# Attention softmax: when the row sums are inverted, and on which engine

## The chip, the cores and the metric

One core of a Trainium2 chip. The metric is the device time of one execution in microseconds (us), the median of three. PE is the matrix engine, with PEld its weight loads; DVE, ACT and POOL are the vector, scalar and GpSimd engines; SP issues most of the DMAs. Each engine works through its own queue in the order in which it was written and waits where an operand isn't ready, so what stands behind a waiting instruction waits too.

## The reference

Causal attention with a decay bias over 4 batches of 8 heads, 576 rows of 64, followed by a gated MLP and a routed mixture of experts. The part at hand:

```python
scores = np.where(causal, -1000000000.0, scores + np.minimum(bias, 0.0))
scores = scores - np.max(scores, axis=-1, keepdims=True)
attn = np.exp(scores)
attn = attn / (np.sum(attn, axis=-1, keepdims=True) + 1e-09)
return np.matmul(attn, v).astype(np.float32)
```

## The kernel before

Attention runs over 32 heads g and, in each, over 5 query tiles i (128 rows each, the last one 64), so 160 tiles (g, i). Tile i has 128(i+1) columns of keys, the last one 576. For one tile:

- S: PE multiplies query and key rows into PSUM (`emit_S`, line 726).
- minimum: DVE copies the negated scores to the tile E, adds the mask and keeps the row minimum (line 424; for i = 4 in two halves, a and b).
- exponent: ACT takes the exponent in place and leaves the row sums in column i of `lsum` (line 432).
- add, reciprocal, scale: POOL adds 1e-9 to the sums (line 436), DVE inverts them (line 437), POOL multiplies E by them (line 440).
- T: PE transposes E (`emit_T`, line 458), ACT or DVE copies the result out of PSUM (lines 463 to 468).
- PV: PE multiplies by the values (`emit_PV`, line 490): the first two tiles of a head together, then the other three.

`A_steps(4)` holds a tile back for four tiles: T of tile (g, i) is written behind S of the fourth tile after it. E has one buffer for each i (two for i = 0). On top of that the early heads share the engines with other work: `split_f64` takes apart the first MLP weights (DMA, then lines 608 and 614 on ACT, 609, 612 and 615 on DVE, 613 on POOL), `emit_cum` makes the bias rows in head 4 (lines 230 to 239, on DVE and ACT), `emit_X` splits a pair of finished heads on POOL (lines 513 and 514), and from about 105 us on the MLP of a finished batch runs between the heads.

The order on each queue isn't the order of the program text: a scheduler sets it, by its own estimate of when each instruction is ready and by the place in the text. An instruction that is given as being behind another one (`behind`) stays behind it, and that alone makes it wait for nothing.

Of the kernel before, what the change touches and what calls it, by code (L numbers as in the profile page):

```python
# [13 lines left out]
ALU = mybir.AluOpType  # L14
# [19 lines left out]
def kernel(  # L34
# [19 lines left out]
    PE, ACT, DVE, POOL, SP = nc.tensor, nc.scalar, nc.vector, nc.gpsimd, nc.sync  # L54
# [7 lines left out]
    NQ = (S + 127) // 128  # L62
    QM = [min(128, S - 128 * i) for i in range(NQ)]
# [6 lines left out]
    NH = B * H  # L70
# [11 lines left out]
    def behind(x, name):  # L82

        tc.add_manual_dep(
            x.ins, name, mybir.DependencyInfo(mybir.DependencyClass.NoSync, mybir.DependencyReason.DATA), reason="after"
        )
# [8 lines left out]
    def ps(tag="ps", bufs=7):  # L95
        t = psum.tile([128, 512], F32, tag=tag, name=tag, bufs=bufs)
        return t
# [18 lines left out]
    def T(pool, shape, dt, tag, bufs=1):  # L116
        _n[0] += 1
        return pool.tile(shape, dt, tag=tag, name=f"{tag}_{_n[0]}", bufs=bufs)
# [42 lines left out]
    def warm_up(n):  # L161

        w = keep_warm[0]
        pw = rs()
        for _ in range(n):
            PE.matmul(pw[0:32].rearrange("p (a c) -> p a c", c=32), lhsT=w, rhs=w.unsqueeze(1).to_broadcast([128, 16, 32]), start=True, stop=True)
# [20 lines left out]
    def slot(z, dt=F32R):  # L187
        x = wsg[:, z, :]
        return x if dt == F32R else x.bitcast(dt)
# [36 lines left out]
    def emit_cum():  # L226
        R = 128 // NH
        s_sb = T(mp, [128, S], F32, "u2", bufs=5)[0:NH]
        dma(s_sb, s.rearrange("b h s -> (b h) s"))
        behind(DVE.tensor_scalar_max(out=s_sb, in0=s_sb, scalar1=0.0), hred[max(hred)].ins.name)  # L230
        cum = s_sb
        DVE.tensor_tensor_scan(out=cum, data0=one[0:NH], data1=s_sb, initial=0.0, op0=ALU.mult, op1=ALU.add)
        for P, i0, z0 in ((128, 0, 6), (NH, R, 8)):
            tmp = T(mp, [128, S], F32, "u2", bufs=5)
            ch = wsg[0:P, z0:z0 + 2, :]
            for a in range(P // NH):
                DVE.tensor_scalar(out=tmp[NH * a:NH * a + NH], in0=cum, scalar1=cum[:, 128 * (i0 + a):128 * (i0 + a) + 1], scalar2=None, op0=ALU.subtract)
            ACT.copy(out=ch[:, 0, :], in_=tmp[0:P])
            DVE.tensor_tensor(out=ch[:, 1, :], in0=tmp[0:P], in1=f32v(ch[:, 0, :]), op=ALU.subtract)
            dma(cum_d[:, NH * i0:NH * i0 + P, :].rearrange("z p s -> p z s"), ch)  # L240
# [22 lines left out]
    def prep_load(p):  # L263
        b, h0 = divmod(2 * p, H)
        for src, nm in ((q, "nq"), (k, "nk")):
            t = T(ap_, [96, 6, 2, D], F32, nm)
            for h in range(2):
                dma(t[:, :, h, :], src[b, h0 + h].rearrange("(r p) d -> p r d", p=96))
            nat[p, nm] = t
# [94 lines left out]
    def prep_asm(g):  # L364
        p, r = divmod(g, 2)
        dst = QK[buf[g]]
        t = Tst[p]
        rs = slice(64 * r, 64 * r + 64)
        dma(dst[64:KX, 3, :], cum_rows[g] if g >= GD else cumr[cblk(g):cblk(g) + 2 * NQ])
        if buf[g] not in selected:  # L370
            selected.add(buf[g])
            dma(dst[64:KX, 2, :], sel[64:KX])
        dma(dst[0:64, 0:3, :], t[rs, 0:3, :])
        dma(dst[0:64, 3, :], t[rs, 1, :])
        dma(dst[64:128, 0:2, :], t[rs, 0:4:3, :])
        if r == 1:
            Tst.pop(p)
# [24 lines left out]
    Et, lsum, hred = {}, {}, {}  # L402

    def emit_S(g, i):
        qk = QK[buf[g]] if g >= ND else None
        M = QM[i]
        N = 128 * i + M
        e = T(ap_, [128, 128 * (i + 1)], F32, f"E{i}", bufs=2 if i==0 else 1) if i < NQ - 1 else E4
        Et[g, i] = e
        nm = T(ap_, [128, 2], F32, "negm", bufs=6)  # L410
        halves = [(0, N)] if N <= 512 else [(0, HS), (HS, N)]
        for hi, (a, z) in enumerate(halves):
            pt = ps()
            n = z - a
            qs = slice(128 * i, 128 * i + M)
            if g < ND:
                t = Tst[g // 2]
                qh, ql = QZ[g]
                pairs = [(qh[:, qs], t[:, 1, a:z]), (qh[:, qs], t[:, 3, a:z]), (ql[:, qs], t[:, 1, a:z]), (slot(6 + g)[:, qs], cumr[:, a:z])]
            else:  # L420
                pairs = [(qk[:, 0, qs], qk[:, 1, a:z]), (qk[0:KX, 2, qs], qk[0:KX, 3, a:z])]
            mm3(pt[0:M, 0:n], pairs, True, True)
            m0 = 512 - 128 * i + a if z == N else 0
            hred[g] = DVE.tensor_tensor_reduce(  # L424
                out=e[0:M, a:z], in0=pt[0:M, 0:n], in1=zmask[0:M, m0:m0 + n], scale=-1.0,
                scalar=BIG if hi == 0 else nm[0:M, 0:1], op0=ALU.add, op1=ALU.min, accum_out=nm[0:M, hi:hi + 1],
            )
        last = len(halves) - 1
        if i == 0:
            lsum[g] = T(ap_, [128, 8], F32, "lsum", bufs=3)  # L430
        l = lsum[g]
        ACT.activation(out=e[0:M, 0:N], in_=e[0:M, 0:N], func=ACTF.Exp, scale=-1.0, bias=nm[0:M, last:last + 1], accum_out=l[0:M, i:i + 1])  # L432
        if i in LG:
            i0 = LG[i]
            c = slice(i0, i + 1)
            POOL.tensor_scalar(out=l[0:M, c], in0=l[0:M, c], scalar1=1e-9, scalar2=0.0, op0=ALU.add, op1=ALU.add)  # L436
            DVE.reciprocal(out=l[0:M, c], in_=l[0:M, c])  # L437
            for x in range(i0, i + 1):
                n = 128 * x + M
                POOL.tensor_scalar(out=Et[g, x][0:M, 0:n], in0=Et[g, x][0:M, 0:n], scalar1=l[0:M, x:x + 1], scalar2=1.0, op0=ALU.mult, op1=ALU.mult)  # L440

    ET = {}
    LG = {z: z for z in range(NQ)}

    def emit_T(g, i):
        e = Et.pop((g, i))
# [88 lines left out]
    def A_steps(LAG):  # L535
        fifo = []
        for n in range(NH * NQ):
            g, i = n // NQ, n % NQ
            p = g // 2
            if i == 0:  # L540
                for x in when:
                    if when[x] == g and g:
                        prep_asm(x)
            if g < len(WU) and WU[g]:
                warm_up(WU[g])
            emit_S(g, i)
            if (g, i) == EC0:
                emit_cum()
            yield 2 * max(107, (128 * i + QM[i]) * 0.42)
            fifo.append((g, i))  # L550
            if (g, i) == RS:
                prep_T(1, 0)
                prep_T(1, 1)
                prep_load(2)
                for x in when:
                    if when[x] == 0:
                        prep_asm(x)
            for p in range(1, NH // 2):
                if (when.get(2 * p) or g) - 1 == g and i in (3, 4):
                    prep_T(p, i - 3)  # L560
                    if i == 4 and p + 1 < NH // 2:
                        prep_load(p + 1)
                    yield 600
            if len(fifo) > LAG:
                yield from after(*fifo.pop(0))
        for x in fifo:
            yield from after(*x)
        emit_PV(NH - 1, 1)
        yield 1230
        emit_X(NH // 2 - 1)  # L570
        done_x[0] += 1
        yield 600
# [4 lines left out]
    def after(g, i):  # L577
        emit_T(g, i)
        yield 110 * (i + 1)
        if i == 2:  # L580
            emit_PV(g, 0)
            yield 860
        if i == 1 and g > 0:
            emit_PV(g - 1, 1)
            yield 1230
        if i == XI and g > 0 and g % 2 == 0:
            emit_X((g - 1) // 2)
            done_x[0] += 1
            yield 600
        if i == 1 and g + 2 < NH:  # L590
            prep_V(g + 2)
# [132 lines left out]
    def mm3(pt, pairs, first_, last_):  # L724
        n = len(pairs)
        ms = [PE.matmul(pt, lhsT=l, rhs=r, start=(first_ and x == 0), stop=(last_ and x == n - 1)) for x, (l, r) in enumerate(pairs)]  # L726
        return ms
# [415 lines left out]
    def fetch(dst, idx, n=NT):  # L1143
        return POOL.indirect_dma_start(
            out=dst, out_offset=None, in_=x2_d[0:n, :], in_offset=bass.IndirectOffsetOnAxis(ap=idx, axis=0),
            bounds_check=n - 1, oob_is_err=False,
        )
# [247 lines left out]
    A_COST, M_COST, O_COST = 45.0, 44.0, 13.0  # L1395
    A_pro()
    A = A_steps(4)
    w = W_steps()
    wg = list(WG)
# [45 lines left out]
    x = fetch(early["xg2"], ids[:, CAP - 1:CAP])  # L1445
# [36 lines left out]
```

## Time and profile before

| what | value |
|---|---|
| median of 3 runs | 802.25 us (800.07 to 802.88) |
| the profiled execution | 803.59 us, its span 801.8 us |
| PE busy | 763.7 us, 95% of the span |
| DVE busy | 532.6 us, 66% |
| ACT busy | 447.0 us, 56% |
| POOL busy | 347.4 us, 43% |

The profiled execution is 1.34 us above the median, and 1.8 us of it lie outside the span. PE is busy nearly all the time; the time that it isn't lies mostly in the first 150 us. A row of the timeline gives start, duration, engine, line, operation, tiles and shape; what stands in brackets is the idle time of that engine just before, and what ended it. A row with x2 is two instructions in a row, merged. The clock that was granted to PE is 1.00 at 2.4 GHz and 0.50 at 1.2 GHz.

### The profile page before, as it was taken

The page shows a single profiled execution, that of the slowest core. Times are in us where ns is not written, and L with a number is a line of the kernel's source. Part 1 is how long each engine was busy: PE and PEld are TensorE (multiplying, and loading weights), DVE is VectorE, ACT ScalarE, POOL GpSimd, SP SyncE. Part 2 cuts the span into 40 slices and gives each one's busy share as a digit, 9 for nine tenths or more (in the row PEclk, how much of TensorE's full clock was granted, in tenths as well). Part 3 has the DMA queues.
Part 4 walks back from the last instruction along what each step waited for, and adds up shares of the span by engine and source line. Part 5 has one row for each costly group of instructions (what it writes and reads, how often), then busy time and mean ns, then how long its engine had stood idle before and what let it go on. Part 6 is the DMA issues. An engine that isn't in the chain of part 4 may idle for free. (4 is left out here: it accounts for less than half of the span.)

```text
span 801.8 us, 14966 instructions
## 1 busy us (share of the span) xinstructions
PE 763.7 (95%) x4744; PEld 643.8 (80%) x4744; DVE 532.6 (66%) x1624; ACT 447.0 (56%) x1077; POOL 347.4 (43%) x629
## 2 busy tenths in 40 slices
PE   9887998999999999999999999998999999999994
PEld 4554687879988888988888877977898988988983
DVE  6668667678698788968788467767454534545530
ACT  5656668687574778745787325413545434545530
POOL 4678663677572568752487401004302121231110
PEclk9988999899999999999999999998999999999998
DMA  6999699974687949578763374312656464665520
GB/s 140 225 229 255 154 243 294 261 201 128 150 170 237 224 106 259 113 161 253 179 140 114 109 250 160 112 61 71 226 179 204 139 209 132 187 192 165 180 81 26
DMA packets 119604, 138.69 MB, mean 173 GB/s; under 512 B 69494, under 2 KB 82934, under 8 KB 119524
## 3 DMA queue, kind: packets, MB, share of 16 engines
q1 hardware_dynamic: 116196, 128.23, 60.2%
q0 software_dynamic: 3328, 9.48, 3.1%
q8 instruction: 39, 0.64, 0.3%
q14 instruction: 41, 0.34, 0.2%
HBM read 89.97 MB, written 22.15 MB: 140 GB/s over the span
## 5 line engine op out<-in xcount | busy, mean ns | idle before, releaser
L1131 DVE TENSOR_TENSOR wp<-wraw,wp 128x1024 fp32r<-128x1024 f32 x63 | 76.6, 1225 | 92.3 <-ACT wp L1130 92.2
L440 POOL TENSOR_SCALAR E<-E,lsum 128x128 f32<-128x128 f32 (+4 forms) x160 | 98.7, 619 | 37.2 <-DVE lsum L437 24.3
L432 ACT ACTIVATE E<-E,negm 128x128 f32<-128x128 f32 (+4 forms) x160 | 97.0, 607 | 23.7 <-DVE negm L424 20.3
L1130 ACT CAST wp<-wraw 128x1024 fp32r<-128x1024 f32 x64 | 66.5, 1048 | 63.4 <-DMA wraw<-in_moe_w_dram 58.7
L726 PE MATMUL ps<-xT,wp 128*128 128x288 f32 (+4 forms) x672 | 99.3, 308 | 0.0
L726 PEld LDWEIGHTS ps<-xT,wp 128*128 128x128 f32 x672 | 98.2, 189 | 0.8
L726 PE MATMUL ps<-wp,hT 128*128 128x512 f32 (+1 forms) x408 | 96.4, 395 | 0.0
L424 DVE CUSTOM_DVE_ANT_0 E<-ps,zmask 128x128 f32<-128x128 f32 (+4 forms) x160 | 75.2, 473 | 21.4 <-PE ps L726 20.6
L726 PEld LDWEIGHTS ps<-wp,hT 128*128 128x128 f32 (+1 forms) x408 | 75.4, 187 | 17.2
L726 PE MATMUL ps<-qk 128*128 128x128 f32 (+3 forms) x354 | 85.6, 337 | 3.5 <-DVE tst L356 1.7
L458 PE MATMUL ps<-ident,E 128*128 128x128 f32 (+1 forms) x480 | 75.2, 264 | 12.4 <-POOL E L440 6.3
L1205 POOL DMA_INDIRECT out_dram<-y,idsr x16 | 20.0, 1250 | 149.0 <-ACT y L1204 117.0
L436 POOL TENSOR_SCALAR lsum<-lsum 128x1 f32<-128x1 f32 (+1 forms) x160 | 38.4, 240 | 102.8 <-ACT E L432 94.1
L458 PEld LDWEIGHTS ps<-ident,E 128*128 128x128 f32 (+1 forms) x480 | 51.2, 140 | 24.5 <-POOL E L440 11.6
L726 PE MATMUL ps<-wsg,vg 128*128 128x288 f32 x448 | 67.7, 301 | 1.6 <-DVE etb L468 1.0
L490 PE MATMUL ps<-etb,vv 128*128 128x320 f32 (+5 forms) x340 | 63.0, 337 | 1.0 <-DVE negm L424 0.8
L726 PEld LDWEIGHTS ps<-wsg,vg 128*128 128x128 f32 x448 | 61.1, 189 | 3.2 <-DVE etb L468 1.3
L726 PEld LDWEIGHTS ps<-qk 128*128 128x128 f32 (+1 forms) x354 | 51.5, 173 | 13.5 <-issue 2.2
L490 PEld LDWEIGHTS ps<-etb,vv 128*128 128x128 f32 (+1 forms) x340 | 49.4, 178 | 14.1 <-issue 5.6
L726 PE MATMUL ps<-xh,w 128*128 128x288 f32 x256 | 57.3, 304 | 0.0
L726 PE MATMUL ps<-w,vg 128*128 128x512 f32 (+1 forms) x216 | 55.1, 399 | 0.0
L726 PE MATMUL ps<-w,xh 128*128 128x512 f32 (+1 forms) x160 | 52.4, 405 | 0.0
(327 smaller groups left out, 1585.4 us busy)
## 6 DMA issues: line engine op xcount, KB each, us to landing
wraw<-in_moe_w_dram SPq DMA_DIRECT2D x64, 512.0 KB
qk<-tst SPq DMA_DIRECT2D x28, 432.0 KB
w<-wv_d SPq DMA_DIRECT2D x16, 512.0 KB
w<-wo_d SPq DMA_DIRECT2D x16, 512.0 KB
qk<-tst SPq DMA_DIRECT2D x28, 288.0 KB
w<-wu_d SPq DMA_DIRECT2D x12, 512.0 KB
nq<-in_q_dram SPq DMA_DIRECT2D x32, 144.0 KB
nk<-in_k_dram SPq DMA_DIRECT2D x32, 144.0 KB
```

Source lines behind the costliest of these rows:

```text
L424: hred[g] = DVE.tensor_tensor_reduce(out=e[0:M, a:z], in0=pt[0:M, 0:n], in1=zmask[0:M, m0:m0 + n], scale=-1.0, scalar=BIG if hi == 0 else ...
L432: ACT.activation(out=e[0:M, 0:N], in_=e[0:M, 0:N], func=ACTF.Exp, scale=-1.0, bias=nm[0:M, last:last + 1], accum_out=l[0:M, i:i + 1])
L436: POOL.tensor_scalar(out=l[0:M, c], in0=l[0:M, c], scalar1=1e-9, scalar2=0.0, op0=ALU.add, op1=ALU.add)
L440: POOL.tensor_scalar(out=Et[g, x][0:M, 0:n], in0=Et[g, x][0:M, 0:n], scalar1=l[0:M, x:x + 1], scalar2=1.0, op0=ALU.mult, op1=ALU.mult)
L458: PE.transpose(pt[:, j * M:(j + 1) * M], e[0:M, 128 * j:128 * (j + 1)], ident[0:M, 0:M])
L490: PE.matmul(pt[0:128 if wide else 64, a:n], lhsT=l, rhs=et[0:kk, z, j, a:n] if g >= F4 else f32v(et[0:kk, 0, j, a:n]), start=(j == 0 and n ...
L726: ms = [PE.matmul(pt, lhsT=l, rhs=r, start=(first_ and x == 0), stop=(last_ and x == n - 1)) for x, (l, r) in enumerate(pairs)]
L1130: c = ACT.copy(out=w[:, 0, :], in_=r)
L1131: a = (POOL if (e, j) == (0, KD) else DVE).tensor_tensor(out=w[:, 1, :], in0=r, in1=f32v(w[:, 0, :]), op=ALU.subtract)
L1205: POOL.indirect_dma_start(out=of[:, :], out_offset=bass.IndirectOffsetOnAxis(ap=idx[0:n], axis=0), in_=y[0:n], in_offset=None, bounds_chec ...
```

## The change

The add goes from POOL to DVE, and add, reciprocal and scale are written one tile later: for tile (g, i) they are issued in the step of the next tile, and the add is put behind the next tile's minimum on DVE. Behind the last tile of the last head one call flushes what is left.

```diff
-        if i in LG:
-            i0 = LG[i]
-            c = slice(i0, i + 1)
-            POOL.tensor_scalar(out=l[0:M, c], in0=l[0:M, c], scalar1=1e-9, scalar2=0.0, op0=ALU.add, op1=ALU.add)
-            DVE.reciprocal(out=l[0:M, c], in_=l[0:M, c])
-            for x in range(i0, i + 1):
-                n = 128 * x + M
-                POOL.tensor_scalar(out=Et[g, x][0:M, 0:n], in0=Et[g, x][0:M, 0:n], scalar1=l[0:M, x:x + 1], scalar2=1.0, op0=ALU.mult, op1=ALU.mult)
+        unscaled.append((g, i))
+        scale_rows(LS, hred[g])
+
+    unscaled = []
+
+    def scale_rows(n, red):
+
+        while len(unscaled) > n:
+            g, i = unscaled.pop(0)
+            M = QM[i]
+            N = 128 * i + M
+            e = Et[g, i][0:M, 0:N]
+            l = lsum[g][0:M, i:i + 1]
+            x = DVE.tensor_scalar(out=l, in0=l, scalar1=1e-9, scalar2=0.0, op0=ALU.add, op1=ALU.add)
+            behind(x, red.ins.name)
+            DVE.reciprocal(out=l, in_=l)
+            POOL.tensor_scalar(out=e, in0=e, scalar1=l, scalar2=1.0, op0=ALU.mult, op1=ALU.mult)
 
     ET = {}
-    LG = {z: z for z in range(NQ)}
+    LS = 1
...
+        scale_rows(0, hred[NH - 1])
         for x in fifo:
             yield from after(*x)
```

The work of PE, ACT and SP stays the same; POOL has 160 instructions less and DVE 160 more. The scheduler also gives many of the others a new place. Three places of this follow. Line numbers of the changed kernel are up to 10 higher: 446, 448 and 449 are its add, reciprocal and scale, and 474, 618, 619, 622, 623 and 625 are 465, 608, 609, 612, 613 and 615 of before.

Place A, DVE in head 1, from the minimum of tile (1, 3) (128x512) on. Tile `vg` holds weights that a DMA brings. Before:

```order
L424 ISA E_89_496,negm_497<-ps,zmask_73 128x512
L424 ISA negm_497 128x1
L437 RECIPROCAL lsum_414<-lsum_414 128x1
L356 SCALAR_TENSOR_TENSOR tst_508<-ps,tst_508 128x288
L465 COPY etb_461<-ps 128x5x64
L359 TENSOR_TENSOR tst_508<-ps,tst_508 128x288
L609 TENSOR_SCALAR vg_420<-vg_420 128x512
L424 ISA E_32_104,negm_531<-ps,zmask_73 64x288
L424 ISA negm_531 64x1
L437 RECIPROCAL lsum_414<-lsum_414 128x1
```

Now:

```order
L424 ISA E_89_493,negm_494<-ps,zmask_73 128x512
L424 ISA negm_494 128x1
L446 TENSOR_SCALAR lsum_411<-lsum_411 128x1
L619 TENSOR_SCALAR vg_417<-vg_417 128x512
L356 SCALAR_TENSOR_TENSOR tst_505<-ps,tst_505 128x288
L474 COPY etb_458<-ps 128x5x64
L448 RECIPROCAL lsum_411<-lsum_411 128x1
L622 SCALAR_TENSOR_TENSOR vg_417<-vg_417 128x512
L424 ISA E_32_104,negm_528<-ps,zmask_73 64x288
```

The weight step (609, now 619) moved ahead of 356, of the copy of `etb` and of the reciprocal of tile (1, 2); 359 moved behind the minimum (1, 4a). The reciprocal of tile (1, 3), the last row of before, now comes 15 rows after the rows shown, behind the second half of the tile and the next two weight steps (619).

Place C, POOL in head 3, from the split of a weight (613, now 623) to the scale of tile (3, 4) (64x576). Before:

```order
L613 TENSOR_TENSOR vg_600<-vg_600,g_104_602 128x512
L440 TENSOR_SCALAR E_123_758<-E_123_758,lsum_715 128x256
L436 TENSOR_SCALAR lsum_715<-lsum_715 128x1 x2
L440 TENSOR_SCALAR E_127_779<-E_127_779,lsum_715 128x384
L440 TENSOR_SCALAR E_129_795<-E_129_795,lsum_715 128x512
L613 TENSOR_TENSOR vg_724<-vg_724,g_119_726 128x512
L436 TENSOR_SCALAR lsum_715<-lsum_715 64x1
L391 TENSOR_SCALAR vv_755<-vt_105 128x64
L436 TENSOR_SCALAR lsum_886<-lsum_886 128x1
L613 TENSOR_TENSOR vg_733<-vg_733,g_121_735 128x512
L440 TENSOR_SCALAR E_32_104<-E_32_104,lsum_715 64x576
```

Now:

```order
L623 TENSOR_TENSOR vg_721<-vg_721,g_119_723 128x512
L449 TENSOR_SCALAR E_123_755<-E_123_755,lsum_712 128x256
L449 TENSOR_SCALAR E_127_776<-E_127_776,lsum_712 128x384
L623 TENSOR_TENSOR vg_730<-vg_730,g_121_732 128x512
L391 TENSOR_SCALAR vv_752<-vt_105 128x64
L449 TENSOR_SCALAR E_129_792<-E_129_792,lsum_712 128x512
L623 TENSOR_TENSOR vg_888<-vg_888,g_143_890 128x512
L449 TENSOR_SCALAR E_32_104<-E_32_104,lsum_712 64x576
```

The four adds are gone and the splits stand one weight earlier; two of them are still ahead of the scale (3, 4).

Place D, DVE in heads 4 and 5, where `emit_cum` takes its differences (237). Before:

```order
L232 SCALAR_TENSOR_TENSOR u_155_991<-u_38_144,u_155_991 32x576
L437 RECIPROCAL lsum_1022<-lsum_1022 128x1
L237 TENSOR_SCALAR u_156_995<-u_155_991 32x576
L437 RECIPROCAL lsum_886<-lsum_886 64x1
L237 TENSOR_SCALAR u_156_995<-u_155_991 32x576 x3
L237 TENSOR_SCALAR u_157_1003<-u_155_991 32x576
```

Now:

```order
L232 SCALAR_TENSOR_TENSOR u_155_988<-u_38_144,u_155_988 32x576
L446 TENSOR_SCALAR lsum_883<-lsum_883 64x1
L237 TENSOR_SCALAR u_156_992<-u_155_988 32x576 x4
L237 TENSOR_SCALAR u_157_1000<-u_155_988 32x576
L448 RECIPROCAL lsum_883<-lsum_883 64x1
```

The reciprocal of tile (4, 4) (64x1) moved from behind the first of the five differences to behind the last. On POOL the pair's split (513, 514, now 522, 523) moved from behind the scale of that tile to ahead of it.

## Rows read from the trace of the kernel before

**Rows 1.** The page's first part: busy time, share of the span and instructions of each engine.
```profile
PE 763.7 (95%) x4744; PEld 643.8 (80%) x4744; DVE 532.6 (66%) x1624; ACT 447.0 (56%) x1077; POOL 347.4 (43%) x629
```

**Rows 2.** By stage: stretch, length, PE, PEld, DVE, ACT, POOL busy, PE's clock, DMA, GB/s.
```profile
20.00:105.00 85.00, 72.76 (x403) 49.67 (x401) 59.64 (x205) 53.00 (x145) 62.49 (x106) 0.90 0.88 216
...
150.00:420.00 270.00, 267.03 (x1842) 233.74 (x1841) 217.92 (x767) 187.68 (x513) 164.40 (x339) 1.00 0.74 182
```

**Rows 3.** The same for a stretch of 5 us.
```profile
65.00:70.00 5.00, 4.70 (x13) 2.29 (x13) 4.83 (x16) 2.18 (x6) 4.64 (x8) 0.50 1.02 335
```

**Rows 4.** PE's waits from 20 to 105 us: total us, times, longest.
```profile
PE ps L458 <- POOL E L440: 6.3, 4, 3.4
```

**Rows 5.** Groups of instructions on POOL and DVE: busy us, mean ns of one, idle before.
```profile
L436 POOL TENSOR_SCALAR lsum<-lsum 128x1 f32<-128x1 f32 (+1 forms) x160 | 38.4, 240 | 102.8 <-ACT E L432 94.1
L783 DVE TENSOR_SCALAR mv<-mv 128x1 f32<-128x1 f32 x16 | 2.4, 149 | 0.3
```

**Rows 6.** Line 436 alone, by stage: stretch, length, POOL busy.
```profile
20.00:105.00 85.00, 9.82 (x40) 0.90 0.88 216
```

**Rows 7.** DVE's waits from 0 to 450 us.
```profile
DVE lsum L437 <- POOL lsum L436: 18.5, 34, 1.5
```

**Rows 8.** Timeline of DVE, 28 to 36 us.
```profile
28.86 0.46 DVE L356 SCALAR_TENSOR_TENSOR tst<-ps,tst 128x288 fp32r<-128x288 f32 x1 [1.53 <-ACT tst L355]
...
29.63 0.45 DVE L359 TENSOR_TENSOR tst<-ps,tst 128x288 fp32r<-128x288 f32 x1
30.62 0.43 DVE L609 TENSOR_SCALAR vg<-vg 128x512 int32<-128x512 int32 x1 [0.54 <-DMA vg<-in_moe_w_in_dram]
...
35.46 0.18 DVE L659 CAST wgl<-gl 128x36 fp32r<-128x36 f32 x1
```

**Rows 9.** Timeline of PE, 31 to 92 us.
```profile
31.47 2.27 PE L490 MATMUL ps<-etb,vv 128*64 128x320 f32 x10 [0.83 <-DVE negm L424]
...
38.70 0.52 PE L458 MATMUL ps<-ident,E 64*128 64x64 f32 x5 [1.75 <-POOL E L440]
...
41.73 0.47 PE L458 MATMUL ps<-ident,E 128*128 128x128 f32 x1 [1.84 <-DMA qk<-tst]
...
42.91 4.32 PE L490 MATMUL ps<-etb,vv 128*64 128x320 f32 x10
...
63.42 0.52 PE L458 MATMUL ps<-ident,E 64*128 64x64 f32 x5 [3.36 <-POOL E L440]
...
66.34 4.32 PE L490 MATMUL ps<-etb,vv 128*64 128x320 f32 x10
...
74.29 0.52 PE L458 MATMUL ps<-ident,E 64*128 64x64 f32 x5
...
79.18 0.41 PE L458 MATMUL ps<-ident,E 128*128 128x128 f32 x2 [1.48 <-DVE negm L424]
...
85.94 0.52 PE L458 MATMUL ps<-ident,E 64*128 64x64 f32 x5 [0.86 <-POOL E L440]
...
87.93 3.96 PE L490 MATMUL ps<-etb,vv 128*64 128x320 f32 x10
```

**Rows 10.** Timeline of POOL, 20 to 76 us.
```profile
20.40 1.25 POOL L440 TENSOR_SCALAR E<-E,lsum 128x384 f32<-128x384 f32 x2
...
53.58 0.52 POOL L436 TENSOR_SCALAR lsum<-lsum 128x1 f32<-128x1 f32 x2
55.45 3.25 POOL L440 TENSOR_SCALAR E<-E,lsum 128x384 f32<-128x384 f32 x2 [1.35 <-DVE lsum L437]
...
60.65 0.21 POOL L436 TENSOR_SCALAR lsum<-lsum 128x1 f32<-128x1 f32 x1
60.94 1.27 POOL L613 TENSOR_TENSOR vg<-vg,g 128x512 int32<-128x512 int32 x1
...
74.17 1.79 POOL L514 TENSOR_TENSOR xl<-xf,xh 128x576 fp32r<-128x576 f32 x1
```

**Rows 11.** Timeline of DVE, 66 to 72.5 us.
```profile
69.11 2.50 DVE L237 TENSOR_SCALAR u<-u 32x576 f32<-32x576 f32 x4
```

## The prediction

> **What bounds the kernel now.** I began with the busy shares [rows 1]: PE is busy 763.7 of 801.8 us, so only what shortens or lengthens PE's idle time, or its clock, can show. The table by stage [rows 2] says where that is: from 150 to 420 us PE is busy 267.03 of 270 us. From 20 to 105 us, in the first nine heads, PE is busy 72.76 of 85 us, its clock is 0.90, and POOL, at 62.49 us, is the next busiest. There the list of waits names the scale on POOL as what PE's transposes waited for longest, 6.3 us in four waits [rows 4]. The timeline [rows 9] shows them one by one: T of tile (1, 4) waits 1.75 us until 38.70, T(2, 0) 1.84 us until 41.73 (the row names a DMA; its own scale ended just then), T(3, 4) 3.36 us until 63.42, T(5, 1) 1.48 us until 79.18, T(5, 4) 0.86 us until 85.94. They cost more than themselves. Behind the third the granted clock is at 1.2 GHz, 0.50 from 65 to 70 us [rows 3]: the ten matmuls of PV take 4.32 us at 66.34, 2.27 us at full clock at 31.47, so 2.05 us more. Behind the first two they take the same 4.32 us, at 42.91; behind the last two they take 3.96 us, 1.69 us more [rows 9].
>
> **The engines' bills.** POOL loses 160 adds of 240 ns, 38.4 us [rows 5]. DVE gains 160 adds. The same form, a 128x1 sum with a constant, is in the trace: line 783, 149 ns [rows 5], so 160 x 0.149 = 23.8 us. DVE loses its waits for POOL's adds, 18.5 us [rows 7], and may wait for ACT's exponent in their place. Neither bill is PE's: from 150 to 420 us DVE is busy 217.92 of 270 us [rows 2], even all 23.8 us would leave it 28 us idle there, and T comes four tiles after S. I charge 1.0 us for DVE answering PE later in that stretch and 0.5 us at the end of the last head, where nothing covers it. Neither has a row; the bounds are 0 and the 3 us that PE is idle there altogether, as if each idle moment doubled. I take the low half because one tile's delay is a quarter of that reserve.
>
> **Place A, heads 1 and 2.** The order puts the first weight step, 609, ahead of 356, of the `etb` copy and of the reciprocal (1, 2). That step waits for its DMA until 30.62 [rows 8], and before, these three and 359 ran ahead of it, three of them from 28.86 to 30.08, that is 1.22 us of work. Now this work lies behind 30.62, and the reciprocal (1, 3), which ran right behind the first half of the next minimum, stands behind everything that before ended with line 659 at 35.64 [rows 8]. Add 1.22 us and two short instructions of 0.15 us, and take off 0.48 us that DVE idled there: some 36.7 us. The POOL scale of (1, 3) and then, behind one more split and the scale (2, 0), that of (1, 4) follow; splits take 1.27 us [rows 10]. Counted on in the same way, the scale (1, 4) ends near 41.8, and T(1, 4) starts 3.1 us later than at 38.70. But T(2, 0), whose own 1.84 us of waiting is then past, follows after 1.2 us of PE's work, near 43.0 in place of 41.73. **+1.3 us**; the bounds are 0 (the scheduler's new order costs nothing that PE waits for) and +3.1 us (T(2, 0) waits as before).
>
> **Place C, head 3.** POOL's road to the scale (3, 4) loses two adds (0.52 us), the 1.35 us for which it waited for a reciprocal that DVE had queued behind six others (it now stands ahead of the minimum (3, 4a)), and two more adds, each 0.29 us from start to start (60.65 to 60.94 is one) [rows 10]: 0.52 + 1.35 + 2 x 0.29 = 2.45 us. T(3, 4) had waited 3.36 us, so **-2.4 us**, with 0.9 us of the wait left. Waits of about that length (0.83 us at 31.47) have full clock behind them [rows 9], so the slow PV behind it should go: **-2.05 us**. Bounds: both stay (0), or the whole wait goes (-5.4 us).
>
> POOL's scales also take longer when DVE is busy: the pair 128x384 and 128x512 took 3.25 us at 55.45 and 1.25 us at 20.40 [rows 10]. The Trainium skill (SBUF — State Buffer, "Who interferes with whom") has a rule on this that speaks against the change: VectorE and GpSimd share a port pair as an exclusive lock, and a VectorE tensor_scalar can take it. No row here shows a one-element instruction doing so; by the rule each moved add could hold POOL for its 149 ns, 40 x 0.149 = 6.0 us of the 9.82 us that POOL saves from 20 to 105 us [rows 6]; the four adds of place C would give back 4 x 0.149 = 0.6 us, and the sum below would be -1.9 us in place of -2.5. I go by the row: the adds are gone from POOL.
>
> **Place D, head 4.** The reciprocal (4, 4) now stands behind four more of `emit_cum`'s differences, 2.50 us [rows 11]. Head 4 arrives about 1.1 us earlier (+1.3 - 2.4), so the reciprocal comes near 70.3, and the scale could end near 71.2, just when PE, 3.15 us ahead with its clock back, asks for T(4, 4) (74.29 less 3.15) [rows 9]. But on POOL the pair's split now stands ahead of that scale, 1.79 us for its second half alone [rows 10], so I charge **+0.8 us**; the bounds are 0 and the 2.50 us.
>
> **Place E, head 5.** T(5, 1) stays late: its reciprocal now stands behind two long rows of `emit_cum` and a weight step, in place of a split ahead of it on POOL; 0. T(5, 4) had waited 0.86 us; two POOL adds are gone from just ahead of its scale, and a split stands two scales further ahead: **-0.9 us**, and about half of the 1.69 us of slow PV behind it, **-0.8 us**; the bounds are 0 and -2.55 us.
>
> **Sum.** 1.3 - 2.4 - 2.05 + 0.8 - 0.9 - 0.8 + 1.0 + 0.5 = -2.55 us, call it -2.5. The profiled execution took 803.59 us, 1.34 us above the median; it would take 801.1, and the median 802.25 - 2.5 = **799.8 us**. That is under 0.5% (4 us), about what a measurement of this kernel can tell from no change.
>
> **Rivals.**
> 1. *POOL is the whole story.* The new order costs nothing in A and D, and the waits in C, at T(5, 1) and at T(5, 4) go with their slow stretches: -4.45 - 1.48 - 2.55 = -8.5 us, 793.8 us. For it: POOL's 62.49 us beside PE's idle time [rows 2]. Against it: three of the places hang on DVE as much as on POOL.
> 2. *A reciprocal stuck in DVE's queue* (slower). In A, T(2, 0) doesn't absorb the delay (+3.1 us), and the wait at T(4, 4) in D is long enough to drop the clock once more (0.8 + 2.05 us), while the gain in C doesn't come because DVE is late there too: +5.95 us, 808.2 us. It decides as soon as DVE, after the DMA at 30.62, doesn't catch up before head 3. For it: DVE was idle just before that DMA landed and used the time; now it can't. Against it: before, DVE idled 18.5 us for POOL's adds [rows 7].
> 3. *Nothing shows.* The scheduler keeps reciprocals so far behind the minimum that POOL's free time is never used, and gains and losses cancel within 1 us: 802.3 us. The text says one tile later, the order says up to a tile and a half, as for (1, 3) and (4, 4).
>
> **Chances.** Forecast 0.36 (0.06 of it past -4 us), rival 1 0.28, rival 2 0.19, rival 3 0.17 (0.02 of it past +4 us). So faster 0.06 + 0.28 = 0.34, slower 0.19 + 0.02 = 0.21, no change 0.45. The range runs from 793 to 808 us: it takes in about two thirds of rival 1 and half of rival 2, and leaves out less than 0.2. The likeliest case alone, with its bounds, has 797 to 802 us.
>
> **What would show it.** A: T(1, 4) near 42 us and T(2, 0) near 43, the weight step of DVE at 30.6 with the `etb` copy behind it. C: T(3, 4) waits about 1 us, and the PV behind it takes 2.3 us. D: T(4, 4) waits under 1 us, with `emit_cum` ahead of its reciprocal. From 150 to 420 us PE is busy 265 us or more. Wrong would be: a T that waits for the scale over 2 us anywhere, new slow stretches of the clock, or PE idle over 6 us between 150 and 420 us.

## The result and the profile after

The changed kernel took **812.2 us** (median of 7 runs, 806.33 to 815.34); the kernel before, run beside it, 802.25 us. The ratio is **1.013**, with a 95% interval of 1.0108 to 1.0153: 1.3% slower, where 799.8 us and no measurable change had been forecast, and above the range of 793 to 808 us. The profiled execution shown here took 809.52 us with a span of 807.7 us, so it is one of the quicker ones.

The page's first part, busy time and instructions of each engine, changed kernel:

```profile
PE 768.8 (95%) x4744; PEld 647.4 (80%) x4744; DVE 550.2 (68%) x1784; ACT 448.2 (55%) x1077; POOL 303.4 (38%) x469
```

Against [rows 1], POOL is 44.0 us less busy and DVE 17.6 us more, where the forecast had 38.4 and 23.8. The price of an add was right: the 160 adds take 116 to 156 ns each on DVE. None of what POOL saved reached the end. By stage (stretch, length, PE, PEld, DVE, ACT, POOL busy, PE's clock, DMA, GB/s), and for four stretches of 5 us:

```profile
20.00:105.00 85.00, 73.91 (x395) 50.25 (x394) 66.89 (x242) 53.23 (x145) 47.40 (x66) 0.86 0.87 211
150.00:420.00 270.00, 264.19 (x1792) 231.06 (x1791) 219.77 (x830) 179.71 (x490) 136.50 (x233) 0.98 0.71 179
...
55.00:60.00 5.00, 3.67 (x16) 2.45 (x17) 4.93 (x17) 4.34 (x12) 2.39 (x3) 0.54 0.50 143
235.00:240.00 5.00, 4.23 (x20) 3.80 (x21) 3.69 (x17) 1.86 (x5) 2.08 (x4) 0.66 0.28 61
345.00:350.00 5.00, 5.00 (x36) 4.64 (x35) 4.20 (x24) 3.23 (x10) 4.65 (x10) 0.90 1.09 215
350.00:355.00 5.00, 5.00 (x20) 3.85 (x20) 4.25 (x20) 2.72 (x8) 1.78 (x2) 0.50 0.51 92
```

From 150 to 420 us PE is idle 5.8 us in place of 3.0, and its clock is 0.98 in place of 1.00 [rows 2]: two stretches at 1.2 GHz, near 236 and near 350 us, are new. From 20 to 105 us the clock is 0.86 in place of 0.90.

Where the time comes in is read from the start of the five transposes with which each pair of heads ends (line 519, now 528), before and after: 51.12 and 52.65, 74.74 and 76.91, 95.30 and 96.44, 111.99 and 113.34, 215.87 and 216.80, 233.13 and 236.66, 344.56 and 351.46, 384.82 and 393.51, 446.65 and 454.58 us. So the first 216 us cost 0.9 us, and the next 170 us cost 7.8 us more. The four rows for this, before and then after:

```profile
215.87 0.71 PE L519 MATMUL ps<-ident,xf 128*128 128x128 f32 x5
...
384.82 0.71 PE L519 MATMUL ps<-ident,xf 128*128 128x128 f32 x5
```

```profile
216.80 0.71 PE L528 MATMUL ps<-ident,xf 128*128 128x128 f32 x5
...
393.51 0.71 PE L528 MATMUL ps<-ident,xf 128*128 128x128 f32 x5
```

PE's timeline (start, duration, shape; in brackets the idle time ahead and what ended it), changed kernel:

```profile
31.34 0.30 PE L467 MATMUL ps<-ident,E 128*128 128x128 f32 x1 [1.94 <-DVE tst L356]
33.35 4.32 PE L499 MATMUL ps<-etb,vv 128*64 128x320 f32 x10
...
43.12 0.52 PE L467 MATMUL ps<-ident,E 64*128 64x64 f32 x5 [1.61 <-POOL E L449]
...
54.88 0.47 PE L736 MATMUL ps<-wsg 128*64 128x288 f32 x2 [1.21 <-DVE negm L424]
56.69 0.74 PE L343 MATMUL ps<-ident,nq 96*128 96x96 f32 x3 [1.33 <-DVE etb L474]
58.82 3.94 PE L499 MATMUL ps<-etb,vv 128*64 128x320 f32 x10
...
66.22 0.52 PE L467 MATMUL ps<-ident,E 64*128 64x64 f32 x5 [0.42 <-POOL E L449]
68.53 2.27 PE L499 MATMUL ps<-etb,vv 128*64 128x320 f32 x10
...
76.46 0.52 PE L467 MATMUL ps<-ident,E 64*128 64x64 f32 x5 [2.14 <-DVE etb L474]
81.82 4.32 PE L499 MATMUL ps<-etb,vv 128*64 128x320 f32 x10
...
235.77 0.38 PE L932 MATMUL rt<-dg,onesf 5*128 5x5 f32 x2 [1.31 <-DVE lsum L448]
```

The first row is the one to read. T of head 1 waits 1.94 us for line 356, a wait that the kernel before did not have, and the PV behind it takes 4.32 us, where the same PV took 2.27 us [rows 9]. DVE's timeline says why:

```profile
30.40 0.43 DVE L619 TENSOR_SCALAR vg<-vg 128x512 int32<-128x512 int32 x1 [2.73 <-DMA vg<-in_moe_w_in_dram]
30.74 0.45 DVE L356 SCALAR_TENSOR_TENSOR tst<-ps,tst 128x288 fp32r<-128x288 f32 x1
31.11 0.48 DVE L474 COPY etb<-ps 128x320 f32<-128x320 f32 x1
31.51 0.15 DVE L448 RECIPROCAL lsum<-lsum 128x1 f32<-128x1 f32 x1
```

The weight step stands in front and waits 2.73 us for its DMA; before, 356 ran at 28.86 in that time [rows 8]. DVE was free, its queue was not. This is the clearest place, not the dearest: at 216 us the changed kernel is only 0.9 us late.

### The profile page after: what moved, and what is told of

It reads as the page before. It is cut to its first block, busy times and chain, and to the rows that moved or that the text cites. A ratio compares the mean times of both kernels' runs of the same rounds, so it can differ in the third digit from the quotient of the medians.

```text
span 807.7 us, 15032 instructions
## 1 busy us (share of the span) xinstructions
PE 768.8 (95%) x4744; PEld 647.4 (80%) x4744; DVE 550.2 (68%) x1784; ACT 448.2 (55%) x1077; POOL 303.4 (38%) x469
## 5 line engine op out<-in xcount | busy, mean ns | idle before, releaser
L499 PE MATMUL ps<-etb,vv 128*128 128x320 f32 (+5 forms) x340 | 64.9, 343 | 0.0
L736 PEld LDWEIGHTS ps<-w,vg 128*128 128x128 f32 (+1 forms) x216 | 38.9, 189 | 9.6 <-issue 0.4
```

The source lines that it names most:

```text
L499: PE.matmul(pt[0:128 if wide else 64, a:n], lhsT=l, rhs=et[0:kk, z, j, a:n] if g >= F4 else f32v(et[0:kk, 0, j, a:n]), start=(j == 0 and n ...
```

## Experiments

Two theories were set against each other first: the **delay** (one tile later takes PE's reserve) and the **work** (160 more instructions on DVE); a third, the **order**, said that the scheduler's new order of the queues is what costs, whatever it was made for. Each ratio is against the kernel before on the same chip, with its 95% interval. "Held" means that a table of numbers with one edge for each neighbouring pair puts the named engines' instructions in a given order. No run holds the old kernel to its own order; that the edges cost little by themselves is read from the held run without the add below (0.9966):

```diff
+    made = {x.name: x for x in nc.all_instructions()}
+    for engine in ORDER:
+        names = pinned(engine)
+        for a, b in zip(names, names[1:]):
+            tc.add_manual_dep(made[b], a, how, reason="order")
```

### One part at a time, the scheduler free

**Add on DVE, no delay.**

```diff
-    LS = 1
+    LS = 0
```

> The add is on VectorE, but add, reciprocal and scale are issued in the step of their own tile again (LS = 0). Delay theory (the tile's delay takes PE's reserve, the loss follows it): the loss of the changed kernel goes, ratio 0.995 to 1.003. Engine theory (160 adds of 144 ns on VectorE answer PE later): ratio 1.010 to 1.015, as the changed kernel has it. Order theory (every new order moves short waits and clock drops about, whatever the reason for it): anything from 0.995 to 1.015, with PE idle and clock loss at other places than in either kernel.

Measured 814.16 us, **1.0136** (1.0098 to 1.0175): as slow as the whole change. The delay isn't needed for the loss.

**Delay, add on POOL.**

```diff
-            x = DVE.tensor_scalar(out=l, in0=l, scalar1=1e-9, scalar2=0.0, op0=ALU.add, op1=ALU.add)
-            behind(x, red.ins.name)
-            DVE.reciprocal(out=l, in_=l)
+            POOL.tensor_scalar(out=l, in0=l, scalar1=1e-9, scalar2=0.0, op0=ALU.add, op1=ALU.add)
+            behind(DVE.reciprocal(out=l, in_=l), red.ins.name)
```

> The add stays on GpSimd, and add, reciprocal and scale are issued one tile later, the reciprocal behind the next tile's minimum. Delay theory: as slow as the changed kernel or slower, ratio 1.010 to 1.020. Engine theory: 0.998 to 1.003. Order theory: anything from 0.995 to 1.015, without a relation to the delay.

Measured 807.46 us, **1.0056** (1.0034 to 1.0077): between the two.

**No add, no delay** (the add's line left out, LS = 0).

> Leaves out the 1e-9 altogether, no delay: 38.4 us less on GpSimd and nothing more on VectorE. If GpSimd's adds cost PE what its waits for the scale show (6.3 us and the slow clock behind them), the ratio is 0.990 to 0.995. If the waits only move elsewhere (order theory), 0.995 to 1.010. The delay and the engine theories both expect 1.000 or less here.

Measured 805.59 us, **1.0039** (1.0014 to 1.0065). Less work than before, and slower: neither delay nor work can do that, only the order can. The same computation in the old order measured 0.9966 (below).

**Two tiles of delay** (LS = 2).

> As the changed kernel, with add, reciprocal and scale two tiles later in place of one. Delay theory: the loss grows with the delay, ratio 1.025 or more, PE waiting for the scale between 150 and 420 us. Engine theory: as the changed kernel, 1.010 to 1.015. Order theory: anything from 0.998 to 1.02.

Measured 825.01 us, **1.0287** (1.0250 to 1.0325). More delay is worse, but the order changes with it, so this run alone settles nothing.

### The order held

**Add on DVE, everything else in its old place** (the edges above, all engines).

> The add is on VectorE, right ahead of its reciprocal, and every other instruction of every engine is held in the place that it has in the kernel before (a table of numbers gives each engine its order). Work theory (VectorE's 160 adds themselves make it late for PE): as slow as the add on VectorE without the hold, 1.010 to 1.017. Order theory (the loss is in the new order that the scheduler makes for the new costs): the loss goes, 0.993 to 1.002, since GpSimd is 38.4 us freer and VectorE no longer waits 18.5 us for its adds.

Measured 811.25 us, **1.0101** (1.0083 to 1.0119). The work theory was right here: the adds cost even in the old order.

**The old computation in the order of the first experiment** (add on POOL; the edges with that order).

> The computation of the kernel before, add on GpSimd, no delay; but PE, ScalarE, VectorE, SP and GpSimd stand in the order that the scheduler made for the add on VectorE without a delay (which measured 1.0136), GpSimd's adds placed freely among them. Order theory: about as slow as that, 1.008 to 1.018. Work theory: close to the kernel before, 0.998 to 1.004, as VectorE has its old work.

Measured 823.03 us, **1.0240** (1.0208 to 1.0272): worse than that order's own kernel, and above the ranges of both theories. A new order alone can cost 2.4%.

**No add, everything else in its old place.**

> Leaves out the 1e-9, with every other instruction held in the place that it has in the kernel before. It bounds what freeing GpSimd of its 160 adds is worth without a new order. If the waits of PE for the scale, 6.3 us from 20 to 105 us and the slow clock behind them, hang on GpSimd's adds: 0.990 to 0.996. If they hang on other things: 0.997 to 1.001. The order theory expects it below the 1.0039 of the same computation in its own new order. The difference to the held kernel with the add on VectorE is the price of VectorE's 160 adds: 0 to 0.003 by the order theory, 0.01 by the work theory.

Measured 799.78 us, **0.9966** (0.9954 to 0.9978). This is what leaving out POOL's adds is worth in the old order: 2.7 us. That the forecast's sum, -2.5 us, is close to it is chance: the forecast's gains from a freer POOL alone were 2.4 + 2.05 + 0.9 + 0.8 = 6.15 us. The adds on DVE then cost 811.25 - 799.78 = 11.5 us.

**The whole change, with PE, ACT and SP in their old order.**

> The whole change (add on VectorE, one tile later), with PE, ScalarE and SP held in the order of the kernel before; VectorE and GpSimd are ordered by the scheduler. If the loss of the change is in PE's new order: 0.996 to 1.003. If it is in what VectorE and GpSimd do, the delay with it: 1.008 to 1.018.

Measured 813.10 us, **1.0121** (1.0102 to 1.0139): the loss stays, so it isn't in PE's order.

### What an add on DVE costs in the old order

**160 sums on a spare tile, off the chain.**

```diff
             DVE.reciprocal(out=l, in_=l)
+            d = spare[:, i:i + 1]
+            DVE.tensor_scalar(out=d[0:M], in0=d[0:M], scalar1=1e-9, scalar2=0.0, op0=ALU.add, op1=ALU.add)
```

> Leaves out the 1e-9, every instruction held in its old place, as in the run without the add that measured 0.9966; added are 160 sums of the add's form on a spare tile that nothing else reads, one right behind each reciprocal on VectorE. So VectorE has the adds' time, but the chain from exponent to scale is no longer than without them. If VectorE's time itself is what costs (work theory): 1.004 to 1.010. If it is the longer chain from the exponent over add and reciprocal to the scale: 0.996 to 0.999.

Measured 801.12 us, **0.9983** (0.9958 to 1.0008): almost free.

**Adds in heads 0 to 8 alone.**

```diff
+            if g < 9:
+                DVE.tensor_scalar(out=l, in0=l, scalar1=1e-9, scalar2=0.0, op0=ALU.add, op1=ALU.add)
```

> Every instruction held in its old place; the add is on VectorE ahead of its reciprocal in heads 0 to 8 (45 tiles) and left out in heads 9 to 31. The held kernel with all 160 adds measured 1.0101, the one with none 0.9966. If each tile's add costs the same: 0.9966 + 45/160 x 0.0135 = 1.0004. If the first 105 us, where PE waits most, carry the cost (as the prediction's places had it): 1.005 to 1.010. If the stretch from 150 us on carries it: 0.9966 to 0.999.

Measured 803.06 us, **1.0003** (0.9981 to 1.0025): 0.0037 for 45 adds, 0.0135 for 160. That is what the same price for each tile gives (1.0004), and it rules out that the early heads carry the cost. The interval still reaches below 0.999, so it isn't shown that the later heads don't pay more.

So why was the spare sum free? The timeline of DVE in the held kernel with the add, then in the one with the spare sum, at the same place:

```profile
181.77 0.14 DVE L446 TENSOR_SCALAR lsum<-lsum 128x1 f32<-128x1 f32 x1
181.94 0.16 DVE L448 RECIPROCAL lsum<-lsum 128x1 f32<-128x1 f32 x1
182.03 0.47 DVE L477 TENSOR_TENSOR etb<-ps,etb 128x320 fp32r<-128x320 f32 x1
```

```profile
178.45 0.15 DVE L448 RECIPROCAL lsum<-lsum 128x1 f32<-128x1 f32 x1
178.52 0.12 DVE L450 TENSOR_SCALAR spare<-spare 128x1 f32<-128x1 f32 x1
178.57 0.47 DVE L479 TENSOR_TENSOR etb<-ps,etb 128x320 fp32r<-128x320 f32 x1
```

In these rows an instruction that doesn't need its neighbour starts 0.05 to 0.09 us behind it, before that one's 0.12 to 0.16 us are over. The reciprocal needs the add, and starts 0.17 us behind it. Over all 160 tiles the median is 175 ns from the add's start to the reciprocal's. Two runs tell this standstill from the longer chain.

**A spare sum that needs the reciprocal.**

```diff
             DVE.reciprocal(out=l, in_=l)
+            DVE.tensor_scalar(out=spare[0:M, i:i + 1], in0=l, scalar1=1e-9, scalar2=0.0, op0=ALU.add, op1=ALU.add)
```

> Leaves out the 1e-9 in the sums; every instruction held in its old place. Right behind each reciprocal VectorE writes the reciprocal plus 1e-9 to a spare tile that nothing reads: it must wait for the reciprocal just ahead, as the add made the reciprocal wait, so VectorE loses about the same 0.14 us a tile, but the scale on GpSimd needs only the reciprocal. If VectorE's time is what the held add costs (1.0101 against 0.9966): 1.005 to 1.011. If it is the longer chain from exponent to scale: 0.997 to 1.001.

Measured 808.75 us, **1.0081** (1.0054 to 1.0107). Its timeline:

```profile
179.04 0.15 DVE L448 RECIPROCAL lsum<-lsum 128x1 f32<-128x1 f32 x1
179.22 0.15 DVE L449 TENSOR_SCALAR spare<-lsum 128x1 f32<-128x1 f32 x1
179.29 0.48 DVE L478 TENSOR_TENSOR etb<-ps,etb 128x320 fp32r<-128x320 f32 x1
```

**The real add, the pairs taken apart** (in 104 tiles the reciprocal and the instruction behind it change places in DVE's table).

> The add on VectorE, every instruction held in its old place, but in 104 of 160 tiles the reciprocal changes places with the independent instruction behind it, so that it no longer stands right behind its add: the add then keeps VectorE some 0.06 us from start to start in place of 0.175 us, and the chain to the scale is one VectorE instruction (0.1 to 0.7 us) longer. If the wait inside the pair is the cost: 1.000 to 1.005. If the chain is: 1.011 to 1.018.

Measured 804.48 us, **1.0016** (0.9992 to 1.0041). Both agree: the cost is DVE's standstill within the pair, not the chain and not the 0.14 us of the add's own row. How 0.1 us more a tile, on an engine that is idle a third of the time, becomes some 10 us of the whole was not followed.

### Delay and order, apart

**The delay in the old order** (DVE's table with 69 adds and reciprocals moved behind the next minimum; POOL free).

> The add on VectorE; PE, ScalarE and SP held in their old order, VectorE too but for this: in the 69 tiles where add and reciprocal stood ahead of the next tile's minimum they now stand right behind it (in the other 91 the old order has them behind it already). GpSimd is ordered by the scheduler. Against the 1.0101 of the held kernel with the add on VectorE and no delay: if the delay costs PE's reserve, 1.014 or more; if the reserve of four tiles covers it, 1.007 to 1.012; if a minimum that no longer stands behind a waiting add answers PE earlier, below 1.007.

Measured 813.57 us, **1.0112** (1.0082 to 1.0142), against 1.0101 without the delay: no difference.

**The delay with the add on POOL, PE, ACT and SP held.**

> The add stays on GpSimd, and add, reciprocal and scale come one tile later; PE, ScalarE and SP held in their old order, VectorE and GpSimd ordered by the scheduler. The delay alone measured 1.0056 with PE's order free. If the delay itself costs: 1.004 to 1.010. If that 0.0056 was the scheduler's other order of PE: 0.998 to 1.002.

Measured 806.89 us, **1.0048** (1.0025 to 1.0072), as with PE's order free (1.0056). What costs lies on DVE and POOL.

**The delay in the old order, pairs taken apart** (126 of 160).

> PE, ScalarE, SP and VectorE held in their old order, with the add on VectorE and the delay: add and reciprocal behind the next tile's minimum in all tiles, and in 126 of 160 one independent instruction between add and reciprocal. If the delay costs nothing by itself and the pair is the cost, as the held runs without the delay have it (1.0101 with pairs, 1.0016 spaced): 1.000 to 1.004. If the delay costs: 1.007 to 1.013.

Measured 804.76 us, **1.0038** (1.0018 to 1.0057). The whole change with PE, ACT and SP held has the same delay and nearly as many adds with another instruction on the sums right behind them (37 of 160 against 34), and measured 1.0121. What is left between the two is the order on DVE and POOL.

**The changed kernel's order, without its adds.**

> Leaves out the 1e-9; every other instruction of every engine is held in the place that it has in the changed kernel, the delay with it. If the changed kernel's loss comes from its 160 adds on VectorE: 0.996 to 1.001. If it comes from its order, the delay with it: 1.007 to 1.012. By the price per tile of the held runs (0.0017 at 52 ns a tile, 0.0135 at 180 ns) the adds, 66 ns in 121 tiles and 179 ns in 39, would be worth some 0.004, and this run would come at 1.009.

Measured 813.24 us, **1.0140** (1.0112 to 1.0168). This was a miss of the price per tile, which had 1.009: in this order the adds cost nothing that shows (1.0130 with them), the order costs all. Only 39 of the changed kernel's 160 adds have another instruction on the sums right behind them.

The last two runs have no adds and the same order on PE, ACT and SP, the old one.

**The order of DVE and POOL that the change got.**

> Leaves out the 1e-9. PE, ScalarE and SP are held in the order of the kernel before, VectorE and GpSimd in the order that the scheduler gave them for the whole change (the run with 1.0121), the delay with it. If VectorE's and GpSimd's order carries the loss: 1.007 to 1.013. If the adds in it do: 0.996 to 1.001.

Measured 812.49 us, **1.0137** (1.0113 to 1.0162).

**The old order of DVE, each reciprocal behind the next minimum.**

> Leaves out the 1e-9. PE, ScalarE, SP and VectorE are held in the order of the kernel before, but each reciprocal stands behind the next tile's minimum (69 of 160 move); GpSimd is ordered by the scheduler. It differs by the delay alone from the run without adds and without delay (0.9966). If one tile's delay costs nothing: 0.995 to 0.999. If it costs: 1.002 or more.

Measured 799.39 us, **0.9962** (0.9940 to 0.9984). A reciprocal right behind the next minimum costs nothing, and the change's order of DVE, or of POOL with it, costs 13 us. By stage, and the waits of DVE from 20 to 150 us and of PE from 20 to 105 us (total, times, longest), first with the change's order, then with the old one:

```profile
20.00:105.00 85.00, 69.93 (x404) 49.38 (x402) 61.59 (x210) 52.97 (x145) 50.33 (x67) 0.92 0.90 217
150.00:420.00 270.00, 263.41 (x1802) 228.78 (x1800) 220.75 (x749) 181.47 (x497) 136.42 (x233) 0.99 0.72 179
DVE vg L617 <- DMA vg<-in_moe_w_in_dram: 7.7, 5, 3.0
DVE vg L617 <- DMA vg<-in_moe_w_out_dram: 1.3, 1, 1.3
PE ps L465 <- POOL E L447: 8.7, 5, 3.1
PE ps L734 <- DVE etb L472: 1.9, 1, 1.9
```

```profile
20.00:105.00 85.00, 73.72 (x411) 49.54 (x410) 63.13 (x215) 55.73 (x155) 50.06 (x66) 0.92 0.92 224
150.00:420.00 270.00, 265.86 (x1830) 232.19 (x1828) 219.93 (x767) 188.06 (x515) 143.41 (x245) 0.99 0.74 183
DVE vg L617 <- DMA vg<-in_moe_w_in_dram: 1.1, 2, 0.6
DVE vg L617 <- DMA vg<-in_moe_w_out_dram: 3.6, 2, 1.9
PE ps L465 <- POOL E L447: 4.5, 3, 2.6
```

With the change's order DVE waits 9.0 us for the DMAs of the two weights in place of 4.7, and PE is busy 3.8 us less in the early heads and 2.5 us less from 150 to 420 us. The order itself fits: in that run's queue of DVE, 30 of the 36 weight steps (609, 612, 615) stand further ahead than in the kernel before, by 2 places in the mean, and 109 of 160 reciprocals further behind; in the changed kernel's own queue, which is another one, it is 35 of 36, by nearly 6 places, and 115 of 160. But the weight steps can't be all of it. At the pair transposes (519) the run with the change's order is 4.7 us behind the other at 74 us, 4.2 us at 212 us and 8.1 us at 381 us, and its last weight step starts at 164 us. Which of these moves costs how much, whether reciprocals that stand still further behind do, and what POOL's share is, was not tried.

## Why the prediction was wrong

By one count more than half of the loss is PE's clock, 5.4 of 9.4 us. The count is span times granted clock, and what is left of the span, worked out for each run and averaged; it takes in idle time at the low clock, which costs nothing, so the second column is an upper bound:

| kernel | span x clock | left, at most lost to the low clock |
|---|---|---|
| before (17 runs) | 781.9 us | 18.6 us |
| changed (7 runs) | 785.9 us | 24.0 us |
| change's order of DVE and POOL, no adds (6) | 790.0 us | 20.5 us |
| old order, delayed, no adds (12) | 781.3 us | 16.1 us |

**The engines' bills: about right, and misleading.** The prediction had 23.8 us for the adds on DVE, and 160 x 0.143 = 22.9 us came. But in a queue the time from start to start counts: 0.07 us where something independent follows, 0.175 us where the reciprocal does.

**Place A: size right by luck, mechanism only half.** The forecast read the new order correctly and counted +1.3 us; by 52.65 us the changed kernel is 1.5 us late. T(1, 4) came at 43.12 (forecast: near 41.8) and T(2, 0) at 44.17 (near 43). The forecast had 356 behind the weight step too; what it missed is that PE waits for 356 until 31.34, with a slow PV behind. That loss, and the waits of T(1, 4) and T(2, 0) that shrank from 1.75 + 1.84 to 1.61 us, happen to leave the size that was forecast.

**Place C: the named wait went, its gain did not.** T(3, 4) waits 0.42 us (forecast 0.9), and its PV takes 2.27 us, as forecast. But 10 us earlier PE now waits 1.21 and 1.33 us for DVE, the clock is 0.54 there, and the PV of that place takes 3.94 us. In front of the minimum for which PE waits first stands a weight step (622, before 612) that takes 2.67 us from 51.55 on, beside the pair's split on POOL, where none of the twelve took more than 0.97 us before. The forecast had -3.15 us for A and C together. T(4, 4) starts 2.17 us later than before (76.46 against 74.29 [rows 9]), and 2.14 us of that are its own wait, so up to there gains and losses only cancel. The step that failed here is "so the slow PV behind it should go": it went elsewhere, since only the waits of the old kernel had been followed. Its reason, that waits of about 0.83 us have full clock behind them, didn't hold in its own rows: T(5, 4) waited 0.86 us, and the PV behind took 3.96 us [rows 9].

**Place D: mis-sized.** Charged +0.8 us, bounds 0 and 2.50. T(4, 4) waits 2.14 us and the next PV takes 4.32. PE's row names the copy of `etb` (474); that copy and the scale of (4, 4) both ended near 76.4, and both stood behind the five differences. DVE's and POOL's rows:

```profile
71.12 0.12 DVE L446 TENSOR_SCALAR lsum<-lsum 64x1 f32<-64x1 f32 x1
71.23 4.26 DVE L237 TENSOR_SCALAR u<-u 32x576 f32<-32x576 f32 x5
75.42 0.15 DVE L448 RECIPROCAL lsum<-lsum 64x1 f32<-64x1 f32 x1
```

```profile
72.07 0.98 POOL L522 TENSOR_SCALAR xh<-xf 128x576 fp32r<-128x576 f32 x1
73.14 1.49 POOL L523 TENSOR_TENSOR xl<-xf,xh 128x576 fp32r<-128x576 f32 x1
75.67 0.74 POOL L449 TENSOR_SCALAR E<-E,lsum 64x576 f32<-64x576 f32 x1 [1.04 <-DVE lsum L448]
```

Five differences took 4.26 us, 0.85 each, where they took 0.62 [rows 11]: three of them now run beside POOL's split. The one that overlaps line 523 took 1.57 us, the last, with POOL idle, 0.51. The Trainium skill (SBUF — State Buffer, "Who interferes with whom") has this lock between VectorE and GpSimd; the prediction weighed it for the adds, where the trace doesn't show it (no add took over 156 ns, and POOL's busy time from 20 to 105 us fell by 15.1 us, more than the 9.82 us of its adds [rows 6]), and not for the long rows, where it does.

**Place E: about right.** The forecast had -1.7 us; between 76.91 and 96.44 us the changed kernel gains 1.0 us, the slow PV behind D included. The list of waits for the scale that it started from has one that wasn't: the row of T(5, 1) names DVE's minimum [rows 9]. That touches rival 1's sum (1.48 us of it) and not the forecast's.

**The 150 to 420 us: the step that decided.** The prediction charged 1.0 us there, with 3 us as bound, because DVE had 28 us idle left and T comes four tiles after S. That step failed: the changed kernel was 0.9 us late at 216.80 and 8.7 us late at 393.51, so 7.8 us, with 2.8 us more idle time of PE and two new stretches at 1.2 GHz. It failed in its reason too: the charge was for DVE's 160 adds and for the delay, and the runs put the loss on neither. The changed kernel's order costs as much without its adds (1.0140), and so does the order that the change gets on DVE and POOL with PE, ACT and SP in their old one (1.0137), while the delay in the old order costs nothing (0.9962). The prediction looked at the new order up to head 5 and took it as harmless behind that without a look. DVE's idle time was no reserve where it could be followed: from 20 to 105 us DVE was idle for 21% of the time, and PE still waited 1.94 us for a row behind a weight step. Which rows make the 7.8 us stays open; one place of it is known, near 236 us (the 5x5 product below). The +0.5 us at the end wasn't there (from 454.58 us on the changed kernel is 2 us shorter).

**The rivals.** Rival 2 had the right sign (808.2 us) and a wait that did come, DVE's queue behind the DMA, but it put the loss into the first five heads, which end 2.2 us late, not 5.95. Rival 1's premise, that POOL's adds cost PE its waits, is bounded now: without them, in the old order, 0.9966, and T(1, 4) and T(3, 4) still wait 2.66 and 2.57 us. Rival 3 had gains and losses cancel within 1 us, which they do at 216 us and not behind it. Of the prediction's own signs of being wrong two came, the new slow stretches and a T that waits over 2 us (T(4, 4)); PE's idle time from 150 to 420 us, 5.8 us, stayed just under its 6. The one tile of delay, which gave the change its name, costs nothing (0.9962 against 0.9966).

## What to carry to other kernels

Where a scheduler sets the queues, a small edit can be two changes: hold the old order and make the edit, then take the new order without the edit, before the edit is blamed or praised. Read a busy share as room only after looking at what stands in front of each queue: at 27.7 us here one instruction that waited 2.73 us for a DMA stopped everything behind it. And don't put an instruction right behind the short one that it needs. The fastest versions here have no add at all, in the old order: a row's sum contains the 1 of its own maximum, and in 32-bit floats 1 + 1e-9 is 1.

## What was not expected of the hardware

- A one-column DVE instruction here costs the queue 0.05 to 0.09 us where the next doesn't need it, and 0.175 us where it does; 160 such pairs made 9.0 to 11.5 us of 800 (808.75 and 811.25 against 799.78). The Trainium skill (VectorE: DVE Perf Modes, "The DRAIN you can't avoid") reports eight chained copies that took the same time with a semaphore after each as with one after the last; for these one-column rows the runs show that a wait for the neighbour does cost.
- A 5x5 product on DVE took 1.60 us, ending with POOL's split, and PE waited 1.31 us for it (PE's row names the reciprocal behind it; the product is the operand, and ended 0.06 us earlier); in the kernel before the same instruction took 0.39 us. The order decides it: without adds it took 2.11 us in the change's order of DVE and POOL and 0.21 us in the old one, though PE, in its old order, didn't wait there. The row of the kernel before, then the rows of DVE and of POOL, changed kernel:

```profile
232.81 0.39 DVE L918 TENSOR_SCALAR dg<-ident,row 5x5 f32<-5x5 f32 x1
```

```profile
234.11 1.60 DVE L928 TENSOR_SCALAR dg<-ident,row 5x5 f32<-5x5 f32 x1
```

```profile
234.30 1.39 POOL L523 TENSOR_TENSOR xl<-xf,xh 128x576 fp32r<-128x576 f32 x1
```

- Near 350 us the granted clock fell to 0.50 with PE busy 5.00 of 5 us from 345 us on and again from 350 us on. Why there, and in no other trace between 340 and 370 us, stays open; the runs of the changed kernel differ by 9 us among themselves, mostly in the clock.
